# State-space mixer and token MLP on one Trainium2 core: shuffles that write every fourth partition instead of every sixteenth, on two queues

## The chip, the core and the metric

The kernel runs on one core of one Trainium2 chip, as one launch. The metric is device time in microseconds, from the launch's own measurement; the profiled execution also has a span, from its first to its last instruction. Five engines work beside each other: TensorE (PE in the profile, its weight loads PEld), VectorE (DVE), ScalarE (ACT), GpSimd (POOL) and SyncE (SP), each with its own instruction stream in order. Data moves with DMAs, issued here by SyncE and ScalarE and carried by the core's 16 DMA engines.

## The reference

Inputs are bf16, with S = 2048 positions and D = 448 channels. Cut to what matters:

```python
def _A_ref(q, k, v, shift_k, ssm_k, ssm_D):
    k_shift = sum over t in 0..3 of k_pad[:, t:t+S] * shift_k[:, 3 - t]
    kv = k_shift * v
    y = irfft(rfft(kv, 2S) * rfft(ssm_k, 2S))[:, :S]     # long causal convolution
    y = y + kv * ssm_D
    return q * y

def _B_ref(x, w1, b1, w2, b2):                            # MLP over the positions
    u = gelu(einsum("bsd,sf->bdf", layernorm(x), w1) + b1)      # F = 1792
    return transpose(einsum("bdf,fs->bds", u, w2) + b2)

h  = A_q + _A_ref(layernorm(A_q), A_k, A_v, ...)
h2 = h + _B_ref(layernorm(h), w1, b1, w2, b2)
```

## The kernel before, in words

Positions are laid out as 128 partitions x 16 rows (R = 16, index r), all in one on-chip tensor called arena; ps is PSUM, eight banks of one 128 x 448 f32 tile each. So every SBUF tensor shows up as "arena" in the profile and is told apart by the line.

The long convolution is a Fourier transform in two stages, done with matmuls, for two inputs: the filter (k, transposed into KT by emit_kT, L817 and L621) and u = kv (V, computed on VectorE in emit_kv, L798 to L807). Stage 1 (emit_stage1, L828): for each r, two matmuls (L832 cosine, L834 sine) into a pair of banks, an evacuation (L839) into one of eight slots of the staging ring WR, and a DMA (L841), the shuffle. A shuffle moves 128 partitions x 1792 B from its slot into eight partitions of T (TK for k, TU for u): r, r + 16, ..., r + 112, in sixteen places j of each. So every row j of T needs all sixteen shuffles. Stage 2 (emit_stage2, L848): for each j four matmuls (L854) with 128 x 128 blocked tables, and an evacuation back into T (L621 and L622 on ScalarE, L624 and L625 on VectorE). Then emit_products_i1: two products on VectorE (L877, L882), eight matmuls of the inverse's first stage (L888), an evacuation into TU and the third kind of shuffle (L893), from TU into TZ, again to partitions j, j + 16, .... The inverse's second stage, emit_i2, adds up in one PSUM bank for each r: V times the skip weights (L951, which needs no shuffle; the weights are multiplied in by L935), then two matmuls on TZ (L953, L955) with tables that emit_ct transposed (L864). Then come gate, sum and layernorm (L958 to L983), and the MLP (L1017, L1025, L1034), whose weights are loaded by ScalarE's queue: W1A (L996) into the place of KH and KT, W1B (L999) into the place of TK, W2 (L1004) into the place of TU and TZ, its first quarter into TU's first ten rows.

The order isn't written out by hand. Every operation is recorded with what it reads and writes, and a planner (_Sched.schedule) simulates the engines with estimated costs, picks at each moment the ready operation of highest priority for each engine, chooses ScalarE or VectorE for an operation that may run on either (FX), and hands out PSUM banks and ring slots. The result is one fixed order for each engine, with semaphore waits put in where needed. An operation that needs a pair of banks takes any two that are free; one that needs a single bank takes any one. All shuffles are issued by SyncE.

The tables are computed on the chip in emit_tables (L630): GpSimd iotas, then VectorE products of integers (L685, L691), masks (L717), and sines on ScalarE; CC, NCC, SS and NSS (L722) are the blocked tables of both stage 2 and the inverse.

Of the kernel before, what the change touches and what calls it, by code (L numbers as in the profile page):

```python
# [71 lines left out]
class _Pool:  # L72
    def __init__(self, n):
        self.n = n
        self.free_t = [0.0] * n
        self.prev = [[] for _ in range(n)]
# [21 lines left out]
class _Sched:  # L98
# [137 lines left out]
    def schedule(self):  # L236
# [41 lines left out]
        def can_acquire(o):  # L278
            need = {}
            for b in o.acq:  # L280
                need[b.pool] = need.get(b.pool, 0) + b.k
            for p, k in need.items():
                if sum(1 for x in p.free_t if x <= t + 1e-6) < k:
# [195 lines left out]
def _build(nc, A_q, A_k, A_v, A_shift_k, A_ssm_k, A_ssm_D, B_w1, B_b1, B_w2, B_b2, out):  # L479
# [52 lines left out]
    o_SM = o_CC + 4 * 256  # L532
    SMALL = o_SM
    NSMALL = 3328

    ctx = ExitStack()
    with ctx:
# [62 lines left out]
        psum = _Pool(8)  # L600
# [6 lines left out]
        def Ppair(b):  # L607
            s0, s1 = b.slots
            return PS[:, s0:s1 + 1:s1 - s0, 0:D]
# [4 lines left out]
        FX = ("act", "dve")  # L614

# [14 lines left out]
        def emit_tables():  # L630
# [6 lines left out]
            o_p = small(16)  # L637
# [3 lines left out]
            pc = view(o_p, [4], i32)  # L641
            pcf = view(o_p + 8, [2], f32)
# [3 lines left out]
            o_dv = o_TT + 4 * (HALF + 128)  # L646
            o_sv = o_dv + 4 * (HALF + 128)
            pi_ = view(o_pi, [HALF + 128], i32)
            dv_ = view(o_dv, [HALF + 128], f32)
            ssm = view(o_sv, [128], f32)  # L650
            csm = view(o_sv + 512, [128], f32)
            msk = view(o_sv + 1024, [128], f32)
            chi = view(o_sv + 1536, [128], i32)
            idi = view(o_sv + 2048, [128], i32)
# [9 lines left out]
            op("pool", lambda e, W: e.iota(idi, [[1, 128]], base=0, channel_multiplier=-1), w=[(o_sv + 2048, 512)],  # L664
# [5 lines left out]
               w=[(o_sv + 1536, 512)], n=128, kind="iota")  # L670
            op("dve", lambda e, W: e.tensor_single_scalar(out=ID, in_=idi, scalar=0.0, op=ALU.is_equal),
               r=[(o_sv + 2048, 512)], w=[(o_ID, 256)], n=128)
            op("dve", lambda e, W: e.tensor_copy(out=IH, in_=ID), r=[(o_ID, 256)], w=[(o_IH, 256)], n=128)
            op("dve", lambda e, W: e.tensor_scalar(out=pc[:, 1:2], in0=pc[:, 0:1], scalar1=15, scalar2=None,
                                                   op0=ALU.bitwise_and), r=[(o_p, 4)], w=[(o_p + 4, 4)], n=1)
            op("dve", lambda e, W: e.tensor_copy(out=pcf[:, 0:1], in_=pc[:, 1:2]), r=[(o_p + 4, 4)],
               w=[(o_p + 8, 4)], n=1)
            op("dve", lambda e, W: e.tensor_scalar(out=pc[:, 1:2], in0=pc[:, 0:1], scalar1=4, scalar2=None,
                                                   op0=ALU.logical_shift_right), r=[(o_p, 4)], w=[(o_p + 4, 4)], n=1)
            op("dve", lambda e, W: e.tensor_copy(out=pcf[:, 1:2], in_=pc[:, 1:2]), r=[(o_p + 4, 4)],  # L680
               w=[(o_p + 12, 4)], n=1)
            for h in range(2):
                n = HALF if h == 0 else HALF + 128
# [6 lines left out]
                if h == 1:  # L690
                    op("dve", lambda e, W: e.tensor_scalar(out=pi_[:, HALF:HALF + 128], in0=cmod,  # L691
                                                           scalar1=pcf[:, 0:1], scalar2=None, op0=ALU.mult),
                       r=[(o_cm, 512), (o_p + 8, 4)], w=[(o_pi + 4 * HALF, 512)], n=128)
# [15 lines left out]
                if h == 1:  # L709
                    op("act", lambda e, W: e.activation(out=ssm, in_=pi_[:, HALF:HALF + 128], func=ACT.Sin,  # L710
                                                        bias=bias[:, 0:1], scale=-SC),
                       r=[(o_pi + 4 * HALF, 512), (o_b, 4)], w=[(o_sv, 512)], n=128)
                    op("act", lambda e, W: e.activation(out=csm, in_=dv_[:, HALF:HALF + 128], func=ACT.Sin,
                                                        bias=bias[:, 1:2], scale=-SC),
                       r=[(o_dv + 4 * HALF, 512), (o_b + 4, 4)], w=[(o_sv + 512, 512)], n=128)
            sch.boost = 1e6
            op("dve", lambda e, W: e.tensor_scalar(out=msk, in0=chi, scalar1=pcf[:, 1:2], scalar2=None,  # L717
                                                   op0=ALU.is_equal), r=[(o_sv + 1536, 512), (o_p + 12, 4)],
               w=[(o_sv + 1024, 512)], n=128)
            for dst, src, so, sgn, k in ((CC, csm, o_sv + 512, 1.0, 0), (NCC, csm, o_sv + 512, -1.0, 1),  # L720
                                         (SS, ssm, o_sv, 1.0, 2), (NSS, ssm, o_sv, -1.0, 3)):
                op("dve", lambda e, W, dst=dst, src=src, sgn=sgn: e.scalar_tensor_tensor(  # L722
                    out=dst, in0=src, scalar=sgn, in1=msk, op0=ALU.mult, op1=ALU.mult),
                   r=[(so, 512), (o_sv + 1024, 512)], w=[(o_CC + 256 * k, 256)], n=128, kind="1x")
# [375 lines left out]
```

## Time and profile before

| | |
|---|---|
| median of 2 runs | 325.86 us (324.25 and 327.46) |
| the profiled execution's own time | 326.04 us |
| its span | 324.2 us |
[...]
| busy, share of the span: PE / DVE / ACT / POOL | 66% / 37% / 34% / 6% |
| moved by DMA | 35.95 MB, mean 111 GB/s |
| chain that ended last: PE / DMA / ACT / DVE | 47% / 31% / 13% / 5% |

How to read it: the span is what the trace covers; 1.8 us of the execution's own time lie outside it. Busy shares are averages over stages with different limits, so the stages are read one by one. In the page's slices the span is cut in 40 equal parts of 8.1 us; a digit is the busy share in tenths. A row of the timeline or of the chain begins with start and duration. Where a line's idle time is given, the name behind the arrow is what ended it.

### The profile page before, as it was taken

The page shows a single profiled execution, that of the slowest core. Times are in us where ns is not written, and L with a number is a line of the kernel's source. Part 1 is how long each engine was busy: PE and PEld are TensorE (multiplying, and loading weights), DVE is VectorE, ACT ScalarE, POOL GpSimd, SP SyncE. Part 2 cuts the span into 40 slices and gives each one's busy share as a digit, 9 for nine tenths or more (in the row PEclk, how much of TensorE's full clock was granted, in tenths as well). Part 3 has the DMA queues.
Part 4 walks back from the last instruction along what each step waited for, and adds up shares of the span by engine and source line. Part 5 has one row for each costly group of instructions (what it writes and reads, how often), then busy time and mean ns, then how long its engine had stood idle before and what let it go on. Part 6 is the DMA issues. An engine that isn't in the chain of part 4 may idle for free.

```text
span 324.2 us, 2484 instructions
## 1 busy us (share of the span) xinstructions
PE 213.5 (66%) x913; PEld 96.8 (30%) x913; DVE 121.5 (37%) x241; ACT 110.0 (34%) x168; POOL 18.3 (6%) x45
## 2 busy tenths in 40 slices
PE   0656434474960766667766446065799999999994
PEld 0511000011330211112222112022354445667772
DVE  8499980006670597001244400049730000003034
ACT  6597434453440333332233223026970122210000
POOL 1000000001020024000000000000530000000000
PEclk9978555559795665555599959559599999999999
DMA  7996555555996000001229579629500000000022
GB/s 199 294 433 176 108 108 111 110 110 114 163 204 175 14 0 0 0 0 27 53 66 259 140 232 271 171 49 381 232 1 0 2 0 0 2 0 28 30 85 86
DMA packets 16279, 35.95 MB, mean 111 GB/s; under 512 B 1100, under 2 KB 10572, under 8 KB 16139
## 3 DMA queue, kind: packets, MB, share of 16 engines
q1 hardware_dynamic: 10250, 21.11, 25.3%
q10 hardware_dynamic: 6016, 14.68, 16.0%
q8 instruction: 7, 0.11, 0.1%
q14 instruction: 6, 0.04, 0.1%
HBM read 22.94 MB, written 1.84 MB: 76 GB/s over the span
## 4 chain that ended last, share of the span: by engine, by line
PE 47%; DMA 31%; ACT 13%; DVE 5%; issue 1%; SPq 1%; DVEq 0%; ACTq 0%
DMA arena<-arena 28%; PE ps L1034 13%; ACT arena L621 10%; PE ps L888 10%; PE ps L854 8%; PE ps L1025 8%; PE ps L1017 6%; DMA arena<-in_A_ssm_k_dram 3%; ACT arena L839 3%; DVE arena L958 2%; DVE arena L961 1%; PE ps L817 1%; DVE arena L1037 1%; SPq L743 0%; DVE arena L624 0%
## 5 line engine op out<-in xcount | busy, mean ns | idle before, releaser
L854 PE MATMUL ps<-arena 128*128 128x448 bf16 x128 | 43.0, 491 | 31.1 <-ACT arena L621 13.6
L621 ACT CAST arena<-ps 128x896 bf16<-128x896 f32 (+1 forms) x32 | 28.2, 881 | 78.7 <-PE ps L854 38.0
L888 PE MATMUL ps<-arena 128*128 128x448 bf16 x128 | 34.4, 424 | 20.8 <-ACT arena L621 20.8
L1034 PE MATMUL ps<-arena 128*128 128x448 bf16 x224 | 45.6, 355 | 0.0
L1037 DVE SCALAR_TENSOR_TENSOR arena<-ps,arena 128x448 bf16<-128x448 f32 x16 | 9.7, 677 | 69.0 <-PE ps L1034 69.0
L839 ACT CAST arena<-ps 128x896 bf16<-128x896 f32 x29 | 25.6, 931 | 29.4 <-DMA arena<-arena 26.2
L1034 PEld LDWEIGHTS ps<-arena 128*128 128x128 bf16 x224 | 31.5, 145 | 13.5 <-ACT arena L1008 3.1
L832 PE MATMUL ps<-arena 128*128 128x448 bf16 x32 | 16.0, 501 | 25.7 <-ACT arena L839 19.9
L854 PEld LDWEIGHTS ps<-arena 128*128 128x128 f16 x128 | 13.2, 119 | 59.8 <-ACT arena L621 23.8
L1025 PE MATMUL ps<-arena 128*128 128x448 bf16 x128 | 29.4, 353 | 0.0
L1017 PE MATMUL ps<-arena 128*128 128x448 bf16 x96 | 23.7, 386 | 5.8 <-DVE arena L983 5.8
L877 DVE TENSOR_TENSOR arena<-arena 128x896 bf16<-128x896 bf16 x16 | 10.0, 625 | 43.5 <-PE ps L888 42.6
L888 PEld LDWEIGHTS ps<-arena 128*128 128x128 f16 x128 | 12.9, 111 | 42.6 <-ACT arena L621 29.9
L1008 ACT ACTIVATE arena<-ps,arena 128x448 bf16<-128x448 f32 x14 | 8.9, 633 | 40.4 <-PE ps L1017 21.1
L958 DVE TENSOR_TENSOR arena<-ps,arena 128x448 bf16<-128x448 f32 x16 | 9.4, 623 | 29.7 <-PE ps L955 29.6
L798 DVE TENSOR_TENSOR arena<-arena 128x1792 bf16<-128x1792 bf16 x16 | 16.5, 1098 | 4.0 <-DMA arena<-in_A_k_dram 4.0
L832 PEld LDWEIGHTS ps<-arena 128*128 128x128 f16 x32 | 3.3, 102 | 46.7 <-ACT arena L839 38.5
L834 PE MATMUL ps<-arena 128*128 128x448 bf16 x32 | 16.5, 516 | 0.0
L1025 PEld LDWEIGHTS ps<-arena 128*128 128x128 bf16 x128 | 12.0, 98 | 12.6 <-ACT arena L1008 2.4
L964 ACT ACTIVATE arena<-arena 128x448 bf16<-128x448 bf16 x16 | 9.2, 576 | 17.3 <-PE ps L953 16.9
L1017 PEld LDWEIGHTS ps<-arena 128*128 128x128 bf16 x96 | 10.1, 106 | 16.3 <-DVE arena L983 6.3
L953 PE MATMUL ps<-arena 128*128 128x448 bf16 x16 | 6.8, 425 | 11.2 <-DMA arena<-arena 11.2
(74 smaller groups left out, 184.4 us busy)
## 6 DMA issues: line engine op xcount, KB each, us to landing
arena<-arena SPq DMA_DIRECT2D x48, 224.0 KB
arena<-in_B_w_dram ACTq DMA_DIRECT2D x5, 2048.0 KB, 9.9
arena<-in_B_w_dram ACTq DMA_DIRECT2D x2, 1536.0 KB, 25.6
arena<-in_A_ssm_k_dram SPq DMA_DIRECT2D x4, 448.0 KB, 7.8
arena<-in_A_k_dram SPq DMA_DIRECT2D x4, 448.0 KB, 12.4
arena<-in_A_v_dram SPq DMA_DIRECT2D x4, 448.0 KB, 13.0
arena<-in_A_q_dram SPq DMA_DIRECT2D x1, 1792.0 KB, 19.0
out_dram<-arena SPq DMA_DIRECT2D x7, 224.0 KB, 1.9
```

What stands on the lines that cost most here:

```text
L621: return e.copy(out=dst(), in_=src())
L798: op("dve", lambda e, W, T=T, i=i, r=r: e.tensor_tensor(out=T[:, i], in0=KH[:, r:r + 4, :], in1=WT, op=ALU.mult), r=[(o_KH + r * DB, 4 * D ...
L832: op("pe", lambda e, W, b=b, r=r: e.matmul(Pb(b, 0), Ct[:, r, :], src[:, r, :], start=True, stop=True), r=[r_C(r), (o_src + r * DB, DB)], ...
L834: op("pe", lambda e, W, b=b, r=r: e.matmul(Pb(b, 1), St[:, r, :], src[:, r, :], start=True, stop=True), r=[r_S(r), (o_src + r * DB, DB)], ...
L839: return e.copy(out=dst, in_=Ppair(b)) if W == "act" else e.tensor_copy(out=dst, in_=Ppair(b))
L854: op("pe", lambda e, W, b=b, bi=bi, tab=tab, ci=ci, st=st, sp=sp, j=j: e.matmul(Pb(b, bi), tab, T[:, j, ci, :], start=st, stop=sp), r=rr, ...
L888: i = op("pe", lambda e, W, b=b, bi=bi, tab=tab, mi=mi, m=m, k=k: e.matmul(Pb(b, bi), tab, MR(m.slots[0])[:, mi, :], start=(k % 4 == 0), s ...
L958: op("dve", lambda e, W, b=b, r=r: e.tensor_tensor(out=V[:, r, :], in0=Pb(b), in1=Q[:, r, :], op=ALU.mult), r=[(o_Q + r * DB, DB)], w=[(o_ ...
L1017: op("pe", lambda e, W, r=r, fc=fc, b=bs[fc]: e.matmul(Pb(b), W1A[:, r, 128 * fc:128 * fc + 128], Q[:, r, :], start=(r == 0), stop=(r == R ...
L1025: op("pe", lambda e, W, r=r, fc=fc, b=b: e.matmul(Pb(b), W1B[:, r, 128 * (fc - n0):128 * (fc - n0) + 128], Q[:, r, :], start=(r == 0), sto ...
L1034: op("pe", lambda e, W, r=r, fc=fc, b=b: e.matmul(Pb(b), W2[:, fc, r:S:R], G[:, fc, :], start=(fc == 0), stop=(fc == NFC - 1)), r=[(o_W2 + ...
L1037: op("dve", lambda e, W, r=r, b=b: e.scalar_tensor_tensor(out=X[:, r, :], in0=Pb(b), scalar=b2c[:, r:r + 1], in1=X[:, r, :], op0=ALU.add, ...
```

## The change

The shuffles of both kinds, L841 and L893, now write partitions 32 (r >> 2) + (r & 3) and then every fourth up to 28 further, eight partitions within one block of 32. Those with even index are issued by SyncE as before, those with odd index by ScalarE. A frequency therefore sits on another partition than before, and the tables follow: stage 2 gets three tables of its own (FC, FS, FNS), with another phase and another mask; CC, NCC, SS and NSS serve the inverse alone. The tables for I2 are transposed from copies with permuted columns, which GpSimd makes in four operations of 128 x 1024 in emit_ct. PSUM pairs must now be aligned neighbours (banks 0 and 1, 2 and 3, ...), and an operation that wants a single bank prefers one whose neighbour is in use. The diff, cut:

```diff
+    def __init__(self, n, pairs=False):
         self.n = n
+        self.pairs = pairs
...
+                if pick(p, k) is None:
                     return False
             return True
+
+        def pick(p, k):
+
+            ok = [x <= t + 1e-6 for x in p.free_t]
+            if k == 1:
+                best = None
+                for i in range(p.n):
+                    if ok[i]:
+                        key = (p.pairs and ok[i ^ 1], p.free_t[i], i)
+                        if best is None or key < best:
+                            best = key
+                return None if best is None else [best[2]]
+            best = None
+            for i in range(0, p.n, 2):
+                if ok[i] and ok[i + 1]:
+                    key = (max(p.free_t[i], p.free_t[i + 1]), i)
+                    if best is None or key < best:
+                        best = key
+            return None if best is None else [best[1], best[1] + 1]
...
-                        fr = sorted((x, i) for i, x in enumerate(p.free_t) if x <= t + 1e-6)[:b.k]
-                        b.slots = sorted(i for _, i in fr)
+                        b.slots = pick(p, b.k)
...
-        CC = view(o_CC, [128], f16)
-        NCC = view(o_CC + 256, [128], f16)
-        SS = view(o_CC + 512, [128], f16)
-        NSS = view(o_CC + 768, [128], f16)
+        BD = [view(o_CC + 256 * k, [128], f16) for k in range(7)]
+        FC, FS, FNS, CC, NCC, SS, NSS = BD
...
-        psum = _Pool(8)
+        psum = _Pool(8, pairs=True)
...
+        SHQ = ("sp", "act")
...
+            ints(1, 0, (SHR, 5), (SHL, 2))
+            ints(2, 0, (AND, 3))
+            ints(3, 0, (SHR, 2), (AND, 7))
+            ints(4, 0, (AND, 15))
+            ints(5, 0, (SHR, 4))
...
+                    for i in range(2):
+                        op("dve", lambda e, W, i=i: e.tensor_scalar(
+                            out=pi_[:, HALF + 128 * i:HALF + 128 * i + 128], in0=cmod,
+                            scalar1=pcf[:, 2 * i:2 * i + 1], scalar2=None, op0=ALU.mult),
+                           r=[(o_cm, 512), (o_p + 24 + 8 * i, 4)], w=[(o_pi + 4 * HALF + 512 * i, 512)], n=128)
...
+            for k, (so, sgn, i) in enumerate(((1, 1.0, 0), (0, 1.0, 0), (0, -1.0, 0), (1, 1.0, 1), (1, -1.0, 1),
+                                              (0, 1.0, 1), (0, -1.0, 1))):
+                src = (ssm, csm)[so][:, 128 * i:128 * i + 128]
+                op("dve", lambda e, W, k=k, src=src, sgn=sgn, i=i: e.scalar_tensor_tensor(
+                    out=BD[k], in0=src, scalar=sgn, in1=msk[:, 128 * i:128 * i + 128], op0=ALU.mult, op1=ALU.mult),
+                   r=[(o_sv + 1024 * so + 512 * i, 512), (o_sv + 2048 + 512 * i, 512)], w=[(o_CC + 256 * k, 256)],
+                   n=128, kind="1x")
...
-                op("sp", lambda e, W, w=w, r=r: e.dma_start(T[r:128:R].rearrange("p j c d -> p j (c d)"),
-                                                            WR(w.slots[0]).rearrange("p c d -> p (c d)")),
+                p0 = 32 * (r >> 2) + (r & 3)
+                op(SHQ[r % 2], lambda e, W, w=w, p0=p0: e.dma_start(
+                    T[p0:p0 + 29:4].rearrange("p j c d -> p j (c d)"),
+                    WR(w.slots[0]).rearrange("p c d -> p (c d)")),
...
+                for bi, tab, ci, st, sp in ((0, FC, 0, True, False), (0, FNS, 1, False, True),
+                                            (1, FS, 0, True, False), (1, FC, 1, False, True)):
...
+            o_cp = o_TT + 16384
+            for k, (tab, o_tab, dst, o_dst) in enumerate(((Ct, o_C, CTt, o_CT), (St, o_S, STt, o_ST))):
                 for h in range(2):
+                    oc = o_cp + 4096 * k + 2048 * h
+                    cp = view(oc, [8, 128], f16)
+                    op("pool", lambda e, W, cp=cp, tab=tab, h=h: e.tensor_copy(
+                        out=cp.rearrange("p r (h f l) -> p r h f l", h=4, f=8),
+                        in_=tab[:, 8 * h:8 * h + 8, :].rearrange("p r (f h l) -> p r h f l", f=8, h=4)),
+                       r=[(o_tab + 2048 * h, 2048)], w=[(oc, 2048)], n=1024)
                     b = _Buf(psum)
                     for i in range(8):
-                        r = 8 * h + i
-                        op("pe", lambda e, W, b=b, i=i, r=r, tab=tab: e.transpose(
-                            out=Pbf(b, 0, f16)[:, 128 * i:128 * i + 128], in_=tab[:, r, :], identity=IH),
-                           r=[(o_tab + 256 * r, 256), (o_IH, 256)], bw=[b], kind="tr")
+                        op("pe", lambda e, W, b=b, i=i, cp=cp: e.transpose(
+                            out=Pbf(b, 0, f16)[:, 128 * i:128 * i + 128], in_=cp[:, i, :], identity=IH),
+                           r=[(oc + 256 * i, 256), (o_IH, 256)], bw=[b], kind="tr")
...
-                op("sp", lambda e, W, j=j: e.dma_start(TZ[j:128:R].rearrange("p r c d -> p r (c d)"),
-                                                       TU[:, j].rearrange("p c d -> p (c d)")),
+                p0 = 32 * (j >> 2) + (j & 3)
+                op(SHQ[j % 2], lambda e, W, j=j, p0=p0: e.dma_start(
+                    TZ[p0:p0 + 29:4].rearrange("p r c d -> p r (c d)"), TU[:, j].rearrange("p c d -> p (c d)")),
```

## Rows read from the trace of the kernel before

**Rows 1.** Page: 40 equal slices of the span; DMA busy in tenths, GB/s moved.

```profile
DMA  7996555555996000001229579629500000000022
GB/s 199 294 433 176 108 108 111 110 110 114 163 204 175 14 0 0 0 0 27 53 66 259 140 232 271 171 49 381 232 1 0 2 0 0 2 0 28 30 85 86
```

**Rows 2.** Chain that ended last, in order of time: start, duration, what.

```profile
29.54 13.60 DMA arena<-arena
...
81.13 23.70 DMA arena<-arena
...
104.91 1.67 PE ps L854 x4
...
179.52 8.83 DMA arena<-arena
...
201.93 11.76 DMA arena<-arena
```

**Rows 3.** Windows: stretch, length, busy per engine, PE clock, DMA share, GB/s.

```profile
16.00:23.00 7.00, 3.41 (x21) 1.24 (x19) 7.00 (x10) 6.16 (x4) 0.00 (x0) 0.75 1.05 432
...
50.00:72.00 22.00, 11.54 (x27) 2.23 (x26) 0.00 (x0) 9.87 (x12) 0.00 (x0) 0.50 0.54 111
...
105.00:146.70 41.70, 26.71 (x69) 7.37 (x68) 18.16 (x47) 14.47 (x16) 6.11 (x10) 0.54 0.01 4
...
219.00:226.00 7.00, 4.44 (x24) 2.15 (x22) 7.00 (x18) 4.55 (x16) 0.00 (x0) 1.00 0.99 378
```

**Rows 4.** Waits of all engines: who for whom, us in total, times, longest.

```profile
ACT arena L839 <- DMA arena<-arena: 26.2, 18, 5.0
```

**Rows 5.** Timeline of stage 1: start, duration, engine, line, what, [idle before].

```profile
23.02 6.62 ACT L839 CAST arena<-ps 128x896 bf16<-128x896 f32 x8
...
73.38 1.09 DVE L839 CAST arena<-ps 128x896 bf16<-128x896 f32 x1 [26.34 <-DMA arena<-arena]
...
79.56 0.91 ACT L839 CAST arena<-ps 128x896 bf16<-128x896 f32 x1 [5.03 <-DMA arena<-arena]
```

**Rows 6.** Timeline behind the last evacuation of stage 1.

```profile
79.57 1.05 ACTq L996 DMA_DIRECT2D arena<-in_B_w_dram  x2
...
80.52 6.81 PE L854 MATMUL ps<-arena 128*128 128x448 bf16 x26 [2.48 <-ACT arena L839]
...
93.07 0.92 PE L951 MATMUL ps<-arena 128*128 128x448 bf16 x4
...
93.83 0.89 PE L864 MATMUL ps<-arena 128*128 128x128 f16 x13
```

**Rows 7.** Timeline of u's stage 2 and the inverse's first stage, PE's rows.

```profile
109.03 0.95 PE L951 MATMUL ps<-arena 128*128 128x448 bf16 x2
...
117.37 1.68 PE L854 MATMUL ps<-arena 128*128 128x448 bf16 x4 [1.00 <-ACT arena L621]
...
163.44 1.69 PE L888 MATMUL ps<-arena 128*128 128x448 bf16 x8 [1.00 <-ACT arena L621]
...
166.13 1.69 PE L888 MATMUL ps<-arena 128*128 128x448 bf16 x8 [1.00 <-ACT arena L621]
```

**Rows 8.** Issues by line: duration ns min, median, max; the loads' landing.

```profile
L841 SPq DMA_DIRECT2D arena<-arena x32: 597/597/1402, 24.0 to 81.1; - x32
...
L999 ACTq DMA_DIRECT2D arena<-in_B_w_dram x2: 377/436/494, 169.0 to 188.8; - x2
...
DMA to landing us min/median/max: 14.4/19.3/24.3
```

**Rows 9.** Page, DMA issues: KB each, us from issue to landing.

```profile
out_dram<-arena SPq DMA_DIRECT2D x7, 224.0 KB, 1.9
```

**Rows 10.** Groups by line and shape: count, busy us, mean ns.

```profile
L722 DVE SCALAR_TENSOR_TENSOR arena<-arena 128x128 f16<-128x128 f32 x4 | 1.0, 288 | 0.5 <-ACT arena L710 0.5
...
L717 DVE TENSOR_SCALAR arena<-arena 128x128 f32<-128x128 int32 x1 | 0.3, 282 | 0.0
...
L669 POOL IOTA arena<- 128x128 int32 x1 | 0.3, 256 | 0.0
```

More of the change, by code (lines that the diff above doesn't have):

```diff
@@ L636, in emit_tables @@
             o_s = small(64)
[L637 removed]
+            o_p = small(48)
             frow = view(o_fr, [128], i32)
@@ L645, in emit_tables @@
             o_pi = o_TT
[L646 to L654, printed above, removed]
+            o_dv = o_TT + 4 * (HALF + 256)
+            o_sv = o_dv + 4 * (HALF + 256)
+            pi_ = view(o_pi, [HALF + 256], i32)
+            dv_ = view(o_dv, [HALF + 256], f32)
+            ssm = view(o_sv, [256], f32)
+            csm = view(o_sv + 1024, [256], f32)
+            msk = view(o_sv + 2048, [256], f32)
+            chi = view(o_sv + 3072, [128], i32)
+            idi = view(o_sv + 3584, [128], i32)
             sch.boost = 3e6
@@ L663, in emit_tables @@
             sch.boost = 2e6
-            op("pool", lambda e, W: e.iota(idi, [[1, 128]], base=0, channel_multiplier=-1), w=[(o_sv + 2048, 512)],
+            op("pool", lambda e, W: e.iota(idi, [[1, 128]], base=0, channel_multiplier=-1), w=[(o_sv + 3584, 512)],
                n=128, kind="iota")
@@ L669, in emit_tables @@
             op("pool", lambda e, W: e.iota(chi, [[1, 8], [0, 16]], base=0, channel_multiplier=0),
[L670 removed]
+               w=[(o_sv + 3072, 512)], n=128, kind="iota")
             op("dve", lambda e, W: e.tensor_single_scalar(out=ID, in_=idi, scalar=0.0, op=ALU.is_equal),
[L672 removed]
+               r=[(o_sv + 3584, 512)], w=[(o_ID, 256)], n=128)
             op("dve", lambda e, W: e.tensor_copy(out=IH, in_=ID), r=[(o_ID, 256)], w=[(o_IH, 256)], n=128)
[L674 to L675 removed]
@@ L676, in emit_tables, with ints @@
[L676 to L681, printed above, removed]
+            def ints(dst, src, a, b=None):
+                op("dve", lambda e, W: e.tensor_scalar(
+                    out=pc[:, dst:dst + 1], in0=pc[:, src:src + 1], scalar1=a[1], scalar2=b[1] if b else None,
+                    op0=a[0], **({"op1": b[0]} if b else {})), r=[(o_p + 4 * src, 4)], w=[(o_p + 4 * dst, 4)], n=1)
@@ new lines, in emit_tables @@
+            SHR, SHL, AND = ALU.logical_shift_right, ALU.logical_shift_left, ALU.bitwise_and
+            ints(1, 0, (SHR, 5), (SHL, 2))
[3 more added lines that the diff above has]
+            ints(5, 0, (SHR, 4))
+            op("dve", lambda e, W: e.tensor_tensor(out=pcf[:, 0:1], in0=pc[:, 1:2], in1=pc[:, 2:3], op=ALU.add),
+               r=[(o_p + 4, 8)], w=[(o_p + 24, 4)], n=1)
+            op("dve", lambda e, W: e.tensor_copy(out=pcf[:, 1:4], in_=pc[:, 3:6]), r=[(o_p + 12, 12)],
+               w=[(o_p + 28, 12)], n=3)
@@ L682, in emit_tables @@
             for h in range(2):
-                n = HALF if h == 0 else HALF + 128
+                n = HALF if h == 0 else HALF + 256
                 sch.boost = 2.5e6 if h == 0 else 1.5e6
@@ L720, in emit_tables @@
[L720 to L724, printed above, removed]
+            for i in range(2):
+                op("dve", lambda e, W, i=i: e.tensor_scalar(out=msk[:, 128 * i:128 * i + 128], in0=chi,
+                                                            scalar1=pcf[:, 2 * i + 1:2 * i + 2], scalar2=None,
+                                                            op0=ALU.is_equal),
+                   r=[(o_sv + 3072, 512), (o_p + 28 + 8 * i, 4)], w=[(o_sv + 2048 + 512 * i, 512)], n=128)
```

42 lines of the change are left out of this document (16 added, 26 removed).

## The prediction, as it was put on record

> **What bounds the kernel now.** I read the page's slices first: from about 28 to 80 us the DMA digit stands at 5 and the rate at 106 to 114 GB/s, slice after slice, while it reaches 433 shortly before and 381 late [rows 1]. A flat level far below what the same engines do elsewhere is a transfer at a limit of its own. The chain of waits, read second, says that this limit sets the end: among its pieces are 13.60 us from 29.54 and 23.70 us from 81.13 of DMA from arena to arena, that is shuffles, and 8.83 and 11.76 us of the same later on [rows 2]. The windows, third, give it per engine [rows 3]. In 50 to 72 us only shuffles run: 111 GB/s at a share of 0.54, so 0.54 x 16 = 8.6 busy engines at 12.9 GB/s each. In 16 to 23 us, where inputs are loaded, each busy engine does 432 / 16.8 = 25.7; in 219 to 226, weights, 378 / 15.8 = 23.9. One shuffle is 128 partitions x 1792 B = 229 kB, so 2.07 us at 111 GB/s, and ScalarE's evacuation takes 0.83 us (6.62 for 8 while the staging ring is fresh) [rows 5]. From the ninth on it waits for a ring slot, that is for DMA: 18 times, 26.2 us [rows 4]. VectorE is done with V at 47.0 and then waits 26.34 us for the same ring, until 73.38 [rows 5]. So stage 1 of k and u is paced by 32 shuffles from 24.0 on: 32 x 2.07 = 66.2 and some 2 to land give 92.2; the last lands at 104.8 [rows 2]. The 12.6 left over are other transfers on the same engines: at 79.5, when a slot came free for the last evacuation, 24 had landed, 3.8 later than 24.0 + 24 x 2.07 + 2 (the input loads), and the last eight then took 25.3 instead of 16.6, 8.7 more, beside W1A's load issued at 79.57 [rows 6].
>
> From 105 to 202 something else bounds: PE and ScalarE take turns. PE's four matmuls (1.68) wait 1.00 for the evacuation before them, and the eight of the inverse do the same [rows 7]. The cause can be read in the order on PE: four and two matmuls of L951 ran before, and each of these six holds a PSUM bank until the last Z shuffle has landed, so one pair of eight banks is left [rows 6, 7]. The change doesn't aim at that.
>
> **The change, part by part.** *The step of four.* Each shuffle still has eight destination rows, so I keep eight engines; what differs is which partitions they write. No row shows such a transfer. Bounds for its time: unchanged at 12.9 GB/s per engine (2.07 us), and at best 25.7 (206 GB/s, 1.12 us). The shuffle differs from the loads in writing eight partitions sixteen apart and in reading SBUF, and the loads also go out by many engines at once; the nearest row is that of the weights, rows of 2 KB like the shuffle's 1.8 KB. I take 23.9 per engine: 191 GB/s, 1.20 us [rows 3].
>
> [...]
>
> *Alternating queues.* SP's issue is 0.60 us [rows 8], well under the shuffle, so SP isn't short of issue time, and I book no gain. The cost is on ScalarE: 16 issues before stage 2 and 8 behind it, at 0.60 each by SP's row. In stage 1 ScalarE then needs (2 x 0.83 + 0.60) / 2 = 1.13 us for each row r, just under the 1.20 of the DMA; so they are nearly level, and about 54 us is when the last evacuation ends (23.0 + 32 x 1.13 = 59, less the four or five that VectorE takes after 47). In the inverse stage ScalarE idles 1.8 us between evacuations, which covers 0.60. Queued behind a waiting issue on ScalarE are its next evacuations, for which PE waits; the issue waits only for the evacuation just ahead, or for VectorE's.
>
> *Tables.* Two more multiplications and masks of 128 columns and three more products, at 0.28 and 0.29 each [rows 10], and some single-element operations: some 2 us more on VectorE before V. V ends near 49 instead of 47; ScalarE reaches V's last four rows at about 23 + 28 x 1.13 = 54, so it is hidden. If ScalarE were faster it would cost those 2 us.
>
> *Copies for the transposes.* Four GpSimd copies of 1024 elements; no row shows one. Below: nothing. Above: 0.26 us for 128 written by an iota, so 2 us each, 8 in all [rows 10], and if each kept VectorE from running, V would end 8 us later, at 57, and cost some 3. GpSimd is idle there and the transposes run after stage 2 of k, 40 us later; I take 0.
>
> *Pairs of PSUM banks.* Pairs are aligned and single banks fill broken pairs. It costs no instruction. It can change the planner's order; that is a rival below.
>
> **What then sets each end.** Stage 1: the shuffles take 32 x (2.07 - 1.20) = 27.8 less; the landing (1.9 for a 224 KB store [rows 9]), the 3.8 for inputs and the 8.7 for W1A (half of its 3.1 MB on these engines is 8.2 us at 191 GB/s) stay, as the same bytes on the same engines. So u's last shuffle lands at 104.8 - 27.8 = 77. Compute might be later: the last evacuation now waits for the 24th landing, 24 + 28.8 + 2 + 3.8 = 58.6, and ends at 59.5 (ScalarE alone would be done at 54); before, PE needed from 80.47 until 94.7 for the rest of k's stage 2, the transposes and the first L951 [rows 5, 6], 15 us with what VectorE adds. That is 74.5, just below 77, so DMA still ends the stage, with 2.5 us to spare: **27.8 us less**.
>
> The wait of 8.83 us: ScalarE holds its evacuation until the shuffle issued at 179.52 has left TU, since W2's first load goes there [rows 2]. It is slow because the W1B load issued at 169.05 (14.4 us to land, as I read the lesser of the two) shares engines that shuffles hold for 2.07 of every 2.68 us [rows 7, 8]. With 1.20 of 2.68 the load has its 1.05 MB through those engines in 5.5 / 0.55 = 10 us, before 179.5; the shuffle then lands in about 3. **5.8 less.**
>
> The tail of 11.76 us: the last Z shuffle competes with 4.2 MB of weights issued at 188.4 and 188.8 (the second takes 24.3 us) [rows 2, 8]. On each of the eight engines lie 262 kB of weights and five shuffles of 29 kB: 405 kB at 23.9 is 17 us, from 182.6 (counted from the old times, less 5.8) to 199.5, and the last evacuation ends at 196.1. Landed at about 200.3, 4.2 after it: **7.5 less**.
>
> The turns of PE and ScalarE, I2 and the MLP stay. Sum against the profiled execution, 326.0 (span 324.2; the median shown is 325.9, so nothing to shift): 326.0 - 27.8 - 5.8 - 7.5 = **285**.
>
> **Rivals.** *The planner lets go of the banks* (two or more pairs for u's stage 2). For it: the six L951 got in while PE waited for the last shuffles; ScalarE's issues move that moment. Against: W1A is planned there still. PE and ScalarE would overlap, 1.70 instead of 2.68 in 32 turns: 31 less, 254 (236 to 268).
>
> *Reading limits.* [...] If reading is as tight as writing, the gain is partial: at 1.60 us, 32 x 0.47 = 15 less, with 3 and 4 at the later waits: 304 (298 to 319). For it: nothing in the rows parts reading from writing. If reading alone was the limit, nothing changes: 326, give or take 5. [...]
>
> *Slower: odd shuffles stand behind weights.* On ScalarE's queue they follow W1A, W1B and W2 loads that take 14.4 to 24.3 us [rows 8]. If a queue is served in order and the rate stays at 2.07, u's last shuffle starts when W1A is done, which shares the engines until about 104.8, and lands two shuffles later (+4), and three Z shuffles start after 188.8 + 24.3 = 213.1 (+6): 336. It decides only when a shuffle stays above about 1.8 us; below that 32 x 0.27 = 9 less and the shorter waits outweigh it. [...]
>
> **How the numbers follow.** Forecast as summed: 0.48, with a range of its own of 268 to 302 (low: PE granted 2.4 GHz instead of the 0.54 of 105 to 146.7 [rows 3] takes 0.75 off 14 turns, and a faster shuffle some more; high: 160 GB/s). Banks let go: 0.14. Reading partly: 0.17. Nothing changes: 0.10. Slower: 0.11. Faster by over 2%, which is about what a measurement of this kernel can tell (the two runs lie 1% apart): 0.48 + 0.14 + 0.17 = 0.79; within: 0.10; slower: 0.11. The range takes in the first three cases, 236 to 319, and leaves out 0.21 less the little of their own edges.
>
> **What would show it.** Between 30 and 60 us: DMA share still near 0.54 but 170 to 210 GB/s; ScalarE's evacuations of stage 1 waiting little for DMA; PE's first u stage 2 matmul near 77; ScalarE's wait before the W2 load under 4 us; the last DMA piece before I2 near 4. Wrong would be: 110 GB/s in that stretch (reading or the engine limits); share near 1 (more engines than eight); PE's turns without the 1.00 us gap (banks let go); a last shuffle on ScalarE's queue landing together with the weights (order in the queue).

## The result and the profile after

The changed kernel takes 262.12 us (two runs, 261.61 and 262.64) where the kernel before takes 325.86: a ratio of 0.804, with an interval of 0.786 to 0.823. The span of its profiled execution is 260.8 us, where before's is 324.2. The prediction was 285 with a range of 236 to 319. So the sign and the range hold, but the forecast gain was 41 us and the measured one is 64, and the gain didn't come from where the sum put it. The sum's own range, 268 to 302, is missed; 262 lies in the whole range only because that takes in the rival *the planner lets go of the banks* (236 to 268), which had a chance of 0.14.

First the page's slices, which answer [rows 1]:

```profile
DMA  7999444545697000367599439700000000001022
GB/s 185 282 386 412 118 155 141 180 136 174 206 252 256 0 0 0 117 192 289 142 348 261 182 125 384 296 2 0 0 3 0 0 0 3 0 0 73 0 106 106
```

The flat stretch at 106 to 114 GB/s is gone. From 26 to 65 us the rate is 118 to 180 with the DMA digit at 4 or 5, so each busy engine moves more, and the engines also stand idle more often. The windows (stretch, length, busy of PE, its weight loads, VectorE, ScalarE and GpSimd, PE clock, DMA share, GB/s) show it, as [rows 3] did:

```profile
29.00:35.00 6.00, 2.38 (x9) 0.46 (x8) 6.00 (x9) 2.80 (x4) 0.00 (x0) 0.99 0.45 129
...
43.00:50.00 7.00, 2.15 (x6) 0.38 (x6) 4.46 (x7) 3.41 (x4) 0.00 (x0) 0.65 0.53 183
...
84.50:98.20 13.70, 11.97 (x61) 5.36 (x60) 12.90 (x21) 7.77 (x9) 1.56 (x3) 1.00 0.00 0
...
128.00:140.00 12.00, 6.75 (x32) 2.80 (x32) 0.85 (x2) 4.50 (x5) 0.00 (x0) 1.00 0.95 275
```

129 GB/s at 0.45 is 17.9 GB/s for each busy engine and 183 at 0.53 is 21.6, against 12.9 before. The third row is u's stage 2: PE is busy for 11.97 of 13.70 us at the full clock (a granted share of 1.00), where before it was busy for 26.71 of 41.70 at 0.54 [rows 3]. PE's timeline shows why:

```profile
77.58 3.99 PE L887 MATMUL ps<-arena 128*128 128x448 bf16 x20 [0.44 <-ACT arena L640]
...
85.66 3.20 PE L887 MATMUL ps<-arena 128*128 128x448 bf16 x16 [0.44 <-ACT arena L640]
...
104.75 0.55 PE L991 MATMUL ps<-arena 128*128 128x448 bf16 x2 [0.43 <-ACT arena L639]
...
112.55 1.69 PE L927 MATMUL ps<-arena 128*128 128x448 bf16 x8 [1.00 <-ACT arena L639]
```

Sixteen matmuls run together, with one gap of 0.44 us, where before four ran and then waited 1.00 [rows 7]. The six skip matmuls (L951 before, L991 here), which hold a PSUM bank each until the last Z shuffle, no longer stand ahead of u's stage 2: the first comes at 104.75, after four rows of the inverse. From there on the old turns of eight matmuls and 1.00 us are back.

The chain of waits, against [rows 2]:

```profile
98.23 5.54 PE ps L927 x29
...
123.26 4.69 DMA arena<-arena
...
140.06 10.14 DMA arena<-arena
```

By stage, with the boundaries from the two chains, windows and timelines: u's stage 2 starts at 84.5 instead of 104.9 (-20.4; one of its rows runs earlier, at 77.6), takes 13.7 instead of 41.8 (-28.1), the inverse's first stage with its wait takes 41.9 instead of 55.2 (-13.3), the tail (the last wait for a shuffle, before the second inverse stage) 10.1 instead of 11.8 (-1.7), and the rest 110.6 against 110.5. Together -63.4, the difference of the spans.

### The profile page after: what moved, and what is told of

It reads as the page before. It is cut to its first block, busy times and chain, and to the rows that moved or that the text cites. A ratio compares the mean times of both kernels' runs of the same rounds, so it can differ in the third digit from the quotient of the medians.

```text
span 260.8 us, 2492 instructions
## 1 busy us (share of the span) xinstructions
PE 190.5 (73%) x913; PEld 95.1 (36%) x913; DVE 134.2 (51%) x258; ACT 100.9 (39%) x159; POOL 23.0 (9%) x49
## 3 DMA queue, kind: packets, MB, share of 16 engines
q1 hardware_dynamic: 6986, 15.61, 18.2%
## 4 chain that ended last, share of the span: by engine, by line
PE 55%; DMA 20%; ACT 14%; DVE 6%; ACTq 2%; issue 1%; SPq 1%; DVEq 0%
PE ps L1074 17%; DMA arena<-arena 16%; PE ps L1065 10%; ACT arena L639 9%; PE ps L927 9%; PE ps L887 8%; PE ps L1057 8%; ACT arena L870 4%; DMA arena<-in_A_ssm_k_dram 4%; DVE arena L998 3%; PE ps L848 2%; DVE arena L1001 2%; ACTq L1036 2%; ACT arena L640 1%; DVE arena L1077 1%
## 5 line engine op out<-in xcount | busy, mean ns | idle before, releaser
L1074 PE MATMUL ps<-arena 128*128 128x448 bf16 x224 | 45.6, 355 | 0.0
L927 PE MATMUL ps<-arena 128*128 128x448 bf16 x128 | 26.5, 354 | 11.9 <-ACT arena L639 11.9
L639 ACT CAST arena<-ps 128x896 bf16<-128x896 f32 (+1 forms) x26 | 22.2, 880 | 32.9 <-PE ps L927 24.2
L887 PE MATMUL ps<-arena 128*128 128x448 bf16 x128 | 28.2, 374 | 6.1 <-ACT arena L639 3.7
L870 ACT CAST arena<-ps 128x896 bf16<-128x896 f32 x30 | 25.5, 946 | 18.1 <-DMA arena<-arena 11.1
L863 PE MATMUL ps<-arena 128*128 128x448 bf16 x32 | 15.4, 489 | 19.5 <-ACT arena L870 15.3
L1065 PE MATMUL ps<-arena 128*128 128x448 bf16 x128 | 29.2, 353 | 0.0
L1057 PE MATMUL ps<-arena 128*128 128x448 bf16 x96 | 23.7, 388 | 5.8 <-DVE arena L1023 5.8
L927 PEld LDWEIGHTS ps<-arena 128*128 128x128 f16 x128 | 11.4, 98 | 26.8 <-ACT arena L639 17.5
L998 DVE TENSOR_TENSOR arena<-ps,arena 128x448 bf16<-128x448 f32 x16 | 9.4, 615 | 22.5 <-PE ps L995 22.4
L887 PEld LDWEIGHTS ps<-arena 128*128 128x128 f16 x128 | 12.1, 102 | 21.8 <-ACT arena L639 5.8
L863 PEld LDWEIGHTS ps<-arena 128*128 128x128 f16 x32 | 3.2, 101 | 36.6 <-ACT arena L870 30.6
L1057 PEld LDWEIGHTS ps<-arena 128*128 128x128 bf16 x96 | 10.1, 106 | 16.7 <-DVE arena L1023 6.9
L865 PE MATMUL ps<-arena 128*128 128x448 bf16 x32 | 15.7, 497 | 0.0
L848 PE MATMUL ps<-arena 112*128 112x112 bf16 x64 | 6.9, 301 | 10.8 <-DVE arena L702 7.2
L993 PE MATMUL ps<-arena 128*128 128x448 bf16 x16 | 6.9, 434 | 9.6 <-DMA arena<-arena 9.6
## 6 DMA issues: line engine op xcount, KB each, us to landing
arena<-in_B_w_dram ACTq DMA_DIRECT2D x2, 1536.0 KB, 14.5
arena<-in_A_q_dram SPq DMA_DIRECT2D x1, 1792.0 KB, 18.1
```

Of the source, the lines that this page charges most:

```text
L639: return e.copy(out=dst(), in_=src())
L863: op("pe", lambda e, W, b=b, r=r: e.matmul(Pb(b, 0), Ct[:, r, :], src[:, r, :], start=True, stop=True), r=[r_C(r), (o_src + r * DB, DB)], ...
L865: op("pe", lambda e, W, b=b, r=r: e.matmul(Pb(b, 1), St[:, r, :], src[:, r, :], start=True, stop=True), r=[r_S(r), (o_src + r * DB, DB)], ...
L870: return e.copy(out=dst, in_=Ppair(b)) if W == "act" else e.tensor_copy(out=dst, in_=Ppair(b))
L887: op("pe", lambda e, W, b=b, bi=bi, tab=tab, ci=ci, st=st, sp=sp, j=j: e.matmul(Pb(b, bi), tab, T[:, j, ci, :], start=st, stop=sp), r=rr, ...
L927: i = op("pe", lambda e, W, b=b, bi=bi, tab=tab, mi=mi, m=m, k=k: e.matmul(Pb(b, bi), tab, MR(m.slots[0])[:, mi, :], start=(k % 4 == 0), s ...
```

## The experiments

Times are medians. The kernels ran on several chips, on which the kernel before took 321.6 to 325.9 us, so ratios to it are compared where they are given, each with its 95% interval. Theories: the partitions written set the rate of a shuffle (the forecast), or those read do; the turns go away by the release of the banks; alternating queues brings or costs something; the tail is late by order in a queue, or by sharing the DMA engines with weights.

**e1, the step alone.** The kernel before, its order and its one queue kept:

```diff
- T[r:128:R]
+ T[32 * (r >> 2) + (r & 3):32 * (r >> 2) + (r & 3) + 29:4]
- TZ[j:128:R]
+ TZ[32 * (j >> 2) + (j & 3):32 * (j >> 2) + (j & 3) + 29:4]
```

> The kernel before, in its own order and with all shuffles on SyncE; only the partitions that both kinds of shuffle write are changed to every fourth. The tables are left as they were, so frequencies meet the wrong tables and the output is not the reference's; the work is the same. Theory A (the step of four makes each shuffle faster, at some 20 GB/s per busy engine as in the changed kernel's stage 1, so 1.4 us instead of 2.07): 32 x 0.67 = 21 less in stage 1 and some 5 to 8 less at the later waits, 296 to 302 us; the 2.68 us turns of PE and ScalarE stay. Theory B (the gain comes from the new order alone): 322 to 328 us, shuffles still at 110 GB/s.

Measured: 280.83 us (275.37 to 284.23 in four runs) against 323.32 (319.28 to 326.62 in seven), below the 296 to 302 expected. Two windows, then the chain:

```profile
40.00:50.00 10.00, 7.75 (x19) 1.24 (x18) 7.18 (x10) 7.65 (x9) 0.00 (x0) 0.50 0.53 199
...
74.00:117.00 43.00, 27.87 (x70) 7.67 (x71) 18.16 (x47) 14.50 (x16) 6.06 (x10) 0.50 0.03 12
```

```profile
74.05 1.66 PE ps L854 x4
...
145.28 4.07 DMA arena<-arena
...
161.45 10.73 DMA arena<-arena
```

199 GB/s is 1.15 us for a shuffle, at the old share of engines; u's stage 2 starts at 74.05. It then keeps its turns, at half clock (0.50), for 43 us. This is the kernel that my sum described, and 280.8 is close to its 285, in part by luck: of the 41.8 us between the two spans (324.2 and 282.4), the start of u's stage 2 gives 30.9 instead of 27.8 and the tail 1.0 instead of 7.5, and the inverse makes up for it, with 44.5 us instead of 55.2, where the sum had taken off 5.8.

**e2, all but the step.** The changed kernel with the old destination rows and its two queues:

```diff
- T[p0:p0 + 29:4]
+ T[r:128:R]
- TZ[p0:p0 + 29:4]
+ TZ[j:128:R]
```

> The changed kernel, same order, same queues, but the shuffles write every sixteenth partition as before; its tables belong to the new partitions, so the output is not the reference's; the work is the same. Theory A: stage 1 is paced by 2.07 us shuffles again, u's stage 2 starts some 20 us later and the tail before the inverse's second stage is longer, 285 to 297 us. Theory B (order alone): 260 to 268 us.

Measured: 283.69 us, 0.886 (0.874 to 0.898), a little below the 285 to 297 expected. A window of stage 1, PE's timeline behind it, and a piece of the chain:

```profile
40.00:50.00 10.00, 5.01 (x12) 0.66 (x10) 6.91 (x9) 4.95 (x6) 0.00 (x0) 0.50 0.51 134
```

```profile
100.90 3.96 PE L887 MATMUL ps<-arena 128*128 128x448 bf16 x20 [0.43 <-ACT arena L639]
```

```profile
131.25 12.09 DMA arena<-arena
```

Without the step the kernel gains about as much as e1 does with it: the turns of stage 2 are gone. Against the changed kernel the step is then worth 18.7 us of span (279.5 against 260.8): the inverse starts 8.0 later without it (106.06 against 98.07) and the wait before W2 is 12.09 instead of 4.69. The rate, 134 at a share of 0.51, is above before's 111, though far below e1's 199 (the changed kernel, in the same order and window, has 168 at 0.51); why it is above was not followed.

**e3, the changed kernel's order, all shuffles issued by SyncE.**

```diff
-             W = o.eng
+             W = "sp" if o.keng == 8 else o.eng
```

> The changed kernel with its planned order kept, but every shuffle issued by SyncE; ScalarE issues only weights. Theory C (an odd shuffle on ScalarE's queue stands behind the weight loads issued before it): the last piece of DMA before the inverse's second stage falls from 10.1 to 4 to 6 us and stage 1 loses ScalarE's issue time, 252 to 258 us. Theory D (weights and shuffles share the engines equally on whichever queue): the tail stays near 10 us, 260 to 264 us.

Measured: 264.88 us, 0.826 (0.817 to 0.834), which overlaps the interval of the change: two queues against one, in the same order of work, were not told apart. In its chain stand the last shuffle of stage 1 and the last Z shuffle, and PE comes to k's stage 2 at 57.40:

```profile
62.61 14.97 DMA arena<-arena
...
142.27 11.15 DMA arena<-arena
```

```profile
57.40 0.93 PE L887 MATMUL ps<-arena 128*128 128x448 bf16 x4
```

No weights are on SyncE's queue, and still the first of these takes 14.97 us to land, beside W1A issued at 58.7 by ScalarE, and the tail is 11.15 where the changed kernel's is 10.14. So order behind weights within a queue doesn't make them. That sharing the engines does was tried for the tail (e7, e9, e10), not for stage 1.

**e4, the banks alone.** The kernel before with its old step and its one queue, aligned pairs of banks, and the skip matmuls planned behind the inverse (the last of these edits is shown):

```diff
-                        r=[(o_ID, 256), (o_V + r * DB, DB)], bw=[b], n=D)
+                        r=[(o_ID, 256), (o_V + r * DB, DB)], bw=[b], n=D, safter=i1_last)
```

> The kernel before with its old step and all shuffles on SyncE, PSUM pairs aligned as in the change, and one thing more: the planner may not place the matmuls of V times the skip weights (six of which held six banks) before the inverse's first stage has ended. Theory E (the turns of PE and ScalarE come from those six banks): u's stage 2 takes about 14 us instead of 42 and the inverse's first stage 30 to 40 instead of 55, stage 1 unchanged, 275 to 290 us. Theory F (the turns have another cause, such as the granted clock): 320 to 327 us.

Measured: 297.90 us (292.34 to 298.96 in four runs) against 323.32, short of the 275 to 290 expected. PE's timeline:

```profile
109.33 3.20 PE L873 MATMUL ps<-arena 128*128 128x448 bf16 x16 [0.43 <-ACT arena L640]
...
127.46 7.72 PE L907 MATMUL ps<-arena 128*128 128x448 bf16 x31 [2.29 <-DVE arena L901]
```

and its chain:

```profile
102.53 5.82 PE ps L873 x17
...
146.78 14.21 DMA arena<-arena
...
164.29 21.16 DMA arena<-arena
```

Stage 2 now runs without turns, from 102.5 to 119.1: with aligned pairs, holding the skip matmuls back is enough for that. The inverse gains less: with its wait it takes 45.4 us instead of 55.2, but behind its first four rows it does four rows in 10.2 us, 2.55 for each against the 2.68 of a turn, since it now waits for VectorE's products. And what the compute gains it loses in part to the slow shuffles: the two DMA waits grow to 14.21 and 21.16.

**e5, the change without the second queue**, planned anew:

```diff
-         SHQ = ("sp", "act")
+         SHQ = ("sp", "sp")
```

> The changed kernel with only the alternation undone: SyncE issues all shuffles, and the planner plans with that. In the plan so made no matmul of V times the skip weights stands ahead of u's stage 2, so several PSUM pairs are free there as in the changed kernel. Theory A (shuffles are faster and steadier on one queue with ScalarE left to evacuate, u's stage 2 starting near 74 us as in the first experiment instead of near 84): 248 to 256 us. Theory G (alternating is itself worth something in stage 1): above 262 us.

Measured: 256.09 us, 0.797 (0.791 to 0.802). A window, PE's timeline and a piece of the chain:

```profile
40.00:50.00 10.00, 8.19 (x19) 1.18 (x18) 7.18 (x10) 7.91 (x10) 0.00 (x0) 0.50 0.53 204
```

```profile
73.74 5.96 PE L887 MATMUL ps<-arena 128*128 128x448 bf16 x20 [6.45 <-DMA arena<-arena]
...
106.67 0.54 PE L991 MATMUL ps<-arena 128*128 128x448 bf16 x2
107.05 7.73 PE L927 MATMUL ps<-arena 128*128 128x448 bf16 x40
```

```profile
127.51 17.23 DMA arena<-arena
```

It isn't told apart from the change (the intervals overlap), but it is faster than e3, which has the same step and the same single queue and differs only in the order that the planner found. With the alternation in the plan, six skip matmuls stand early in the inverse; without it, two. The inverse takes 29.7 us instead of 42.0 and, begun 8.4 earlier, ends at 119.4 instead of 140.1. Most of that is lost again: the last Z shuffle, issued at 127.51, lands at 144.8; SyncE's issues of Z shuffles had taken up to 4.16 us there, with a median of 0.88, where in e3 none took more than 0.61.

**e6, the late weights planned later.** e5 with the skip matmuls held back, and W1B's second half and W2 *planned* behind the Z shuffles (`safter`, an order and no wait; one line of the edit is shown):

```diff
+                        safter=zdma if h else ())
```

> The one before, with the skip matmuls held back until the inverse's first stage has ended and with the second W1B load and all W2 loads planned after the last shuffle into TZ. Theory H (the last shuffles are slow because 4.2 MB of weights share their engines): the wait of ScalarE before W2 goes and the last piece of DMA before the inverse's second stage falls from 10 to 11 us to 3 to 5, 8 to 12 us less than the one before. Theory I (that piece is the shuffles' own backlog): as the one before, within 3 us.

Measured: 257.81 us, 0.802 (0.797 to 0.807), no gain over e5. ScalarE's timeline and the chain say why:

```profile
118.12 0.37 ACTq L1041 DMA_DIRECT2D arena<-in_B_w_dram  x1
```

```profile
126.00 19.39 DMA arena<-arena
```

The second half of W1B went out at 118.12, before SyncE had issued the last Z shuffles (the last one at 126.00). The planned order across the two engines held nothing back here.

**e7, the weights' part of that edit in the changed kernel** (the skip matmuls as they are), whose ScalarE issues every second Z shuffle itself, so that its own order holds the weights back (its last Z shuffle is issued at 139.63, W1B's second half at 140.28):

> The changed kernel with both queues, with the second W1B load and all W2 loads planned after the last shuffle into TZ, nothing else. Theory H: 252 to 256 us. Theory I: 260 to 264 us.

Measured: 254.41 us, 0.792 (0.787 to 0.798). A window and the tail in the chain:

```profile
128.00:140.00 12.00, 7.10 (x34) 2.92 (x34) 1.11 (x2) 4.48 (x5) 0.00 (x0) 1.00 0.34 91
```

```profile
139.63 5.23 DMA arena<-arena
```

Without weights in 128 to 140 us the tail is 5.23 instead of 10.14, and the wait before W2 is gone. In the same window the changed kernel moved 275 GB/s at 0.95, and the kernel before did the same in 188.4 to 202:

```profile
188.40:202.00 13.60, 8.27 (x33) 3.19 (x34) 0.00 (x0) 4.53 (x5) 0.00 (x0) 0.81 0.96 276
```

Both are 18.0 to 18.1 GB/s for each busy engine, with shuffles and weights, W1B's second half and the first piece of W2, mixed. Not every mixture is as slow. In e5, where W1B's halves are issued at 106.88 and 115.63 beside Z shuffles and W2 comes only at 130.74:

```profile
110.00:120.00 10.00, 8.95 (x48) 4.16 (x45) 9.15 (x22) 4.33 (x5) 2.45 (x4) 1.00 0.88 325
```

That is 23.1 for each busy engine. And shuffles alone, issued at intervals as in e7's window above, come to 16.7 (91 over 0.34 of 16).

**e8, the disputed rate by itself.** Behind the changed kernel's own work, eight bursts of 16 transfers of 229 kB, each burst behind the one before. The order: step 16 on one queue; step 4 on one queue; step 4 on two; step 16 on two; eight neighbouring partitions; step 16 read from HBM; step 4 read from HBM; copies that write all 128 partitions.

> The changed kernel, and behind its end eight bursts of sixteen transfers of 229 KB with nothing beside them, each burst after the one before has landed: (1) shuffles to every sixteenth partition on one queue, (2) to every fourth on one queue, (3) to every fourth on two queues, (4) to every sixteenth on two queues, (5) to eight neighbouring partitions, (6) every sixteenth from HBM, (7) every fourth from HBM, (8) plain copies of all 128 partitions. Write side alone limits: per transfer 2.07, 1.15, 1.15, 2.07, 2 to 4, 2.07, 1.15, 0.6 us. Reading limits too: (7) is clearly faster than (2). Two queues cost or bring something of themselves: (3) differs from (2).

Windows inside the eight bursts, in that order:

```profile
262.00:290.00 28.00, 0.00 (x0) 0.00 (x0) 0.00 (x0) 0.00 (x0) 0.00 (x0) 0.50 0.53 107
297.00:312.00 15.00, 0.00 (x0) 0.00 (x0) 0.00 (x0) 0.00 (x0) 0.00 (x0) 0.50 0.52 191
317.00:331.00 14.00, 0.00 (x0) 0.00 (x0) 0.00 (x0) 0.00 (x0) 0.00 (x0) 0.50 0.52 188
340.00:368.00 28.00, 0.00 (x0) 0.00 (x0) 0.00 (x0) 0.00 (x0) 0.00 (x0) 0.50 0.53 114
380.00:430.00 50.00, 0.00 (x0) 0.00 (x0) 0.00 (x0) 0.00 (x0) 0.00 (x0) 0.50 0.54 63
438.00:466.00 28.00, 0.00 (x0) 0.00 (x0) 0.00 (x0) 0.00 (x0) 0.00 (x0) 0.50 0.50 108
474.00:488.00 14.00, 0.00 (x0) 0.00 (x0) 0.00 (x0) 0.00 (x0) 0.00 (x0) 0.50 0.49 207
492.00:502.00 10.00, 0.00 (x0) 0.00 (x0) 0.00 (x0) 0.00 (x0) 0.00 (x0) 0.50 0.92 353
```

With the share of engines fixed near one half (0.49 to 0.54), the rate follows the partitions written: 63, 107 and 191 GB/s for steps of 1, 16 and 4. Reading from HBM leaves step 16 where it was (108 against 107) and lifts step 4 by 8% (207 against 191), so reading SBUF was no limit for the old step and at most a small one for the new. A second queue changes nothing beyond 7% at step 16 (114 against 107) and nothing at step 4 (188 against 191).

**e9 and e10, weights that truly wait.** e5, with the second half of W1B and W2 (e9), or both halves and W2 (e10), waiting for the last Z shuffle by its semaphore; for e10 (e9 has `after=zdma if h else ()` in the first line):

```diff
+                        after=zdma)
...
-                    w=[(o_W2 + c0 * 4096, (c1 - c0) * 4096)], dmab=128 * (c1 - c0) * 4096)
+                    w=[(o_W2 + c0 * 4096, (c1 - c0) * 4096)], dmab=128 * (c1 - c0) * 4096, after=zdma)
```

> The kernel e5 (all shuffles in steps of four on SyncE's queue), and the second half of W1B and the whole of W2 now wait on a semaphore for the last Z shuffle; the first half of W1B is issued as in e5 (106.88 us there), in the middle of the Z shuffles. Theory H (the end of the inverse is late because weights and shuffles share the DMA engines): in e5 the last Z shuffle landed at 144.8 us, 17.2 us after its issue, beside 4.2 MB of W1B and after the queue had backed up on SyncE (one issue of 4.16 us). With 2.1 MB of weights less in that stretch, at the 387 to 410 GB/s that plain loads reach in e5's slices near 120 us, some 5 us are saved against e5: about 251 us; and if W2 was in the way too, down to 244. Rival: SyncE's own queue holds the shuffles back whatever runs beside them, then 255 to 256, as e5. Rival: the weights that now come late are missed by the MLP, then 258 or more, with PE waiting at L1065 or at L1074 for a DMA.

> The same with both halves of W1B and W2 waiting for the last Z shuffle, so that from u's stage 2 to the last Z shuffle nothing but shuffles is on the DMA engines. Theory H: 16 Z shuffles of 229 kB are 3.67 MB, at the 200 to 212 GB/s of e5's slices without weights 17.3 to 18.4 us; first issue near 104.7, so the last lands at 124 to 128 us instead of 144.8, the second inverse stage starts 17 to 21 us earlier, and the kernel takes 235 to 241 us. The weights then have the second inverse stage and the first 96 matmuls of the MLP (22.5 us at L1057) as their cover: W1B's 4.2 MB at 390 GB/s is 11 us, so no wait of PE at L1065. Rival, the last Z shuffle is held by the inverse itself and by SyncE's issues: its landing no earlier than 139, 250 us. Rival, the weights come too late: a DMA wait of PE at L1065 or L1074 that gives back 5 to 15 us, 245 to 255.

Measured: e9 244.44 us, 0.760 (0.754 to 0.766), and e10 241.55 us, 0.753 (0.747 to 0.758). e9's last Z shuffle in its chain, then e10's:

```profile
123.30 9.95 DMA arena<-arena
```

```profile
120.52 6.08 DMA arena<-arena
```

Windows of e10, during the last Z shuffles and behind them, then ScalarE's timeline:

```profile
119.00:126.00 7.00, 0.93 (x4) 0.23 (x4) 1.13 (x3) 0.14 (x1) 0.00 (x0) 0.72 0.48 181
...
126.60:136.00 9.40, 9.35 (x35) 4.25 (x36) 8.27 (x20) 2.26 (x7) 0.00 (x0) 0.69 0.90 327
```

```profile
137.86 3.95 ACTq L1047 DMA_DIRECT2D arena<-in_B_w_dram  x1
...
141.85 0.58 ACT L1009 ACTIVATE arena<-arena 128x448 bf16<-128x448 bf16 x1 [3.33 <-issue]
```

The last Z shuffle lands at 133.3 and 126.6 instead of e5's 144.8. So weights beside the shuffles made most of e5's tail, and both rivals fall: SyncE's queue doesn't hold the shuffles back by itself, and no matmul of the MLP waits for a DMA (in the waits of 126 to 240 us only the inverse's do, 11.8 us in e9 and 6.5 in e10). e10's time is 0.5 above the expected 235 to 241: of 18.2 us that the landing gains, 14.5 arrive, since ScalarE stands in the issue of W2's last piece for 3.95 us and its activations wait behind it. e10 is faster than both kernels; its ratio, 0.753, is 0.05 below the change's, and the intervals lie apart.

## Why the prediction was right and where it was wrong

**What bounds, and the step's term: right.** I took 23.9 GB/s per engine and 1.20 us for a shuffle, and wrote -27.8 for stage 1. e1 measured 1.15 us and u's stage 2 at 74.05 instead of the forecast 77, that is -30.9; e8 measured 23.0 GB/s per engine (191 over 0.52 of 16). The rivals *reading partly* and *nothing changes* fell with e8's second, sixth and seventh rows.

In the changed kernel, however, that term came out as -20.4, and not because of the transfer: u's first row runs at 77.58, near the forecast 77, and what it waits for last is ScalarE and not a DMA. The step that failed is compute's path. The forecast had DMA ending the stage with 2.5 us to spare over compute, which was to be done at 74.5; here compute ends it, at 84.5. Stage 1's last evacuation ends at 67.2 instead of 59.5, which is 7.7 of the 10.0, and the rest of k's stage 2 behind it takes 17.3 instead of 15. Stage 1's shuffles are issued at intervals, with 129 to 183 GB/s, and PE comes to k's stage 2 only at 63.90. PE's timeline, the issue rows and ScalarE's timeline:

```profile
63.90 2.49 PE L887 MATMUL ps<-arena 128*128 128x448 bf16 x8
```

```profile
L873 SPq DMA_DIRECT2D arena<-arena x16: 613/613/1461, 24.5 to 64.6; - x16
L873 ACTq DMA_DIRECT2D arena<-arena x16: 623/910/1681, 28.0 to 67.2; - x16
```

```profile
67.85 4.03 ACTq L1036 DMA_DIRECT2D arena<-in_B_w_dram  x2
71.93 0.92 ACT L640 ACTIVATE arena<-ps 128x896 bf16<-128x896 f32 x1 [3.85 <-issue]
```

ScalarE's shuffle issues are a cause: without them and in the same order, e3's PE comes to k's stage 2 at 57.40. That doesn't bring u's stage 2 forward there, since e3's last shuffle then lands only at 77.6, beside W1A.

**Alternating: no gain, as booked; its price was mis-sized.** I priced ScalarE's issue at SP's 0.60. Its median is 0.91, up to 1.68, and W1A's two issues took 4.03, for which the evacuation behind them waited 3.85. What the alternation did besides is to the plan: e5 against e3. In e5 u's stage 2 starts at 73.74 and not at 84.5, but most of what that and the shorter inverse gain is lost again at its tail. The whole of it was not told from zero, since the intervals of e5 and the change overlap.

**Tables and copies: hidden, as taken.** VectorE is done with V at 47.5, where before it was 47.0; my 2 us were too many. GpSimd's four copies take 1.11 us each, inside the bounds of nothing and 2 us, and GpSimd is done with them by 13.4 us.

**The wait before W2: nearly right.** Forecast 3 us, measured 4.69, and 4.07 in e1.

**The tail: mis-sized.** Forecast 4.2, measured 10.14, and 10.73 in e1. The bytes on the eight engines were my estimate, 405 kB each, and I took them at 23.9 GB/s, a rate of weights alone. In 128 to 140 us a busy engine does 18.1 (275 over 0.95 of 16). At that rate 405 kB take 22.4 us and not 17, an estimate with the mean of all sixteen engines, and from W2's issue at 127.97 to the landing at 150.2 it is 22.2. So 5.4 of the 5.9 us by which the tail was missed are there. The row was to be had before: 276 at 0.96 in 188.4 to 202. e7, e9 and e10 show that the tail goes with the weights (5.23, 9.95 and 6.08, against 10.14 in the change and 17.23 in e5); why this mixture is slower than e5's is open.

**"The turns of PE and ScalarE stay": wrong, and the largest miss.** The rival *the planner lets go of the banks* came in for u's stage 2, at 0.14. It was priced at 0.98 us (2.68 less 1.70) for each of 32 turns, 31 in all. It gave 28.1 in stage 2's 16 turns alone and little in the inverse, whose turns return after four rows. Two things make the 28.1. At full clock a turn of four matmuls would be 0.85 + 1.00, an estimate from the eight that take 1.69 [rows 7], so 16 of them 29.6 instead of 41.8: some 12 are the clock, and the remaining 16 the overlap. e4 shows that the release, with aligned pairs, does it, e2 that it needs no step of four, e1 that the step alone doesn't bring it. The clue in the prediction, that ScalarE's issues shift the moment at which the skip matmuls find a bank, is not needed for it: e5 has none of these issues and has no turns in stage 2 either. Which of the remaining edits, pairs, tables or copies, moved the plan there was not tried. The low end of my sum's range had PE granted 2.4 GHz; no run shows that figure. The traces give the clock as a share, in the mean 0.783 before and 0.900 in the change, and in the kernel before eight matmuls take 1.70 us at 1.00 and 3.18 at 0.50.

**The inverse, -13.3** where the sum had -5.8: 4.1 of it is the wait. The rest is the four rows without turns and the clock, 1.00 in 98.2 to 140.1; how it divides was not parted by a run.

**Slower, odd shuffles behind weights: fell.** With the new rate it had no ground by its own condition, and e3 shows late landings, at the tail too, where no weights are on the shuffles' queue.

So the time is 23 us below the forecast as follows: stage 2's length -28.1, the inverse -7.5 beyond its term, and the other way +7.4 at the start of u's stage 2 and +5.8 at the tail. That is -22.4 of the 22.9; the 0.5 left lies between profiled execution and median.

## What to carry to other kernels

A transfer at a flat rate below what the same engines do elsewhere can be bound by the partitions it writes (e8: 107 and 191 GB/s at shares of 0.53 and 0.52): cost it by rows of the same number of engines, and change the step before the number of queues (e8: a second queue gave 188 for 191). Where an order is planned, a change of durations or queues can reorder work far from it, so price what each scarce buffer's early holder costs before booking that a stall will stay; here it was worth about as much as the step itself (e1 and e2). And a transfer that ends a stage should not share its engines with loads that can come later (the last Z shuffle took 17.23 us in e5 and 6.08 in e10): give those a real wait, since a planned order held nothing between engines (e6: a load issued at 118.12, ahead of the shuffle at 126.00), and take the rate of a mixture from a row of that same mixture.

## What the runs showed of the hardware

- Transfers with eight destination partitions, which keep about half of the DMA engines busy (shares of 0.54, 0.53 and 0.52): 63 GB/s into neighbouring partitions, 107 sixteen apart, 191 four apart within 32 (e8).
- W2's first piece, W1B's second half and shuffles on the same engines reach 18 GB/s per busy engine at a share of 0.95, where weights without shuffles, W1B with W2 behind it on the same queue, do 22.7 (327 over 0.90 of 16 in e10), step-4 shuffles alone, one behind the other, 23.0 (e8), and W1B with step-4 shuffles 23.1 (e5). What makes the first mixture slower was not tried.
- The issue of a transfer held its engine for very different times: 0.37 to 0.38 us for each piece of W2 and 0.61 for most of SyncE's shuffles in the change, but 4.03 for the two pieces of W1A there and 3.95 for one piece of W2 in e10. What made these long was not tried.
